# Turning C and x's last chunk with VectorE and DMAs instead of TensorE, in a gated mix of a state-space layer and an FFN

## The chip, the cores and the metric

The kernel runs on one core of one Trainium2 chip. The metric is the time of one execution on the device, in microseconds, the median of the runs shown. TensorE multiplies matrices into PSUM (eight banks), VectorE and ScalarE work on rows of 128 partitions, POOL (GpSimd) and SP (SyncE) mostly issue DMAs.

## The reference

For 2048 tokens x of width 448 (bf16):

```python
g = sigmoid((x * gate_w).sum(-1, keepdims=True))
Lam_bar = exp(dt * Lam);  B_bar = ((Lam_bar - 1) / Lam)[:, None] * Bmat        # complex
h = Lam_bar * h + B_bar @ x_t                                                  # for each token t
a = 2 * Re(h @ Cmat.T) + x * Dskip
b = silu(x @ w1) @ w2                                                          # 448 -> 1792 -> 448
out = g * a + (1 - g) * b
```

The recurrence over complex h is the only part that goes from token to token.

## The kernel before, in words

The tokens are worked in four chunks of 512 (`CH`), each of four blocks of 128. The 448 complex states lie in seven "slots" of 128 partitions: real parts of three blocks, a mixed slot 3 (64 real, 64 imaginary), imaginary parts of three blocks.

For a chunk tc, TensorE makes x turned by transposes (`x_transposes`, L498 to 518; the first chunk by `x0_transposes`), then two kinds of products with it (`x_products`, L647; all matmuls have line L663): F(tc), 14 tiles of x @ w1, and B(tc), 7 tiles of x with B. A product is cut into 64-row halves that run in pairs. `evict` (L623) takes them from PSUM: F by ScalarE with SiLU into aT, B into U (chunk 0 by VectorE, L640, the others by ScalarE, L642).

`lanes(tc)` (L706) is the recurrence, on VectorE: U is multiplied by COS and SIN (a rotation that turns the complex recurrence into a real one) into H; seven scans (L736) run along the tokens into Gf (float32); Gf is cast to bf16 back into U, by DMAs of POOL (L390) for chunks 0 to 2 and by ScalarE (L746) for chunk 3; then the rotation is undone into H (products with PO, COS; the final subtraction). The carry from chunk to chunk is `gin`.

`ffn2(tb)` (G, L765) multiplies aT by w2 for one block (L774), ScalarE scales it by 1 - g into fe (L780), and a POOL DMA adds it to Tb (L782), which is the x tile itself, holding g * x * Dskip by then. `readout(tb)` (C, L786) multiplies H by CP, seven matmuls (L795), and VectorE adds g times that to Tb (L798); SP stores the block (L801).

CP is C turned and scaled. `readout_weights(k)` turns it on TensorE (L814), ScalarE scales one copy into ct (L822, L825), and VectorE combines them from PSUM (L827, L830). `gates(tc)` (L834) makes g.

The order. `Plan` keeps all operations with what they read and write; `order` simulates them with a cost each and fixes each engine's queue beforehand. TensorE's queue is the order in which the program adds its operations. For the other engines the ready operation that can start first is taken, and of several the one with the lowest `prio`. SP also works in that planned order. Each engine runs its own queue in order, so a waiting instruction holds all behind it. TensorE's order is, with the readout weights as cp:

```python
F0 and B0, B1;  cp(0) G(0,1) cp(1,2) G(2,3) cp(3)
F1, one tile of F2, B2 (x chunk 2 turned in it);  G(4..7);  C(0..3)
rest of F2, B3, F3 (x chunk 3 turned in it);  C(4..7);  G(8..11);  C(8..11);  G(12..15);  C(12..15)
```

Buffers: there are four H (H2 first holds C as loaded, H3 first holds B), and two U, taken in turn by the chunks.

Of the kernel before, what the change touches and what calls it, by code (L numbers as in the profile page):

```python
# [24 lines left out]
NFILL = 2  # L25
XCOL = [0, 128, 256, 320]
# [22 lines left out]
class Op:  # L49
    __slots__ = ("i", "eng", "fn", "reads", "writes", "cost", "prio", "sem",  # L50
                 "deps", "succ", "ps_w", "ps_r", "start", "end", "bytes", "tag", "own")


class Plan:
# [5 lines left out]
    RATE = {"pool": 300e3, "hw": 300e3}  # L60
    LAP = {"dve": 0.08, "act": 0.09}
# [6 lines left out]
    def add(self, eng, fn, reads=(), writes=(), cost=0.2, prio=50, sem=None, nbytes=0, tag=""):  # L68
# [28 lines left out]
        o.own = False  # L97
        o.start = o.end = None
# [5 lines left out]
    def order(self):  # L104
# [14 lines left out]
        def earliest(o):  # L119
            t = 0.0  # L120
            for d in o.deps:
                p = ops[d]
                t = max(t, p.end + (self.HOP[p.eng] if p.eng != o.eng else 0.03))
            for x in o.ps_w:
                if x.bank is None:
                    b = place(x.n, t)
                    if b is None:
                        return None
                    t = max(t, max(banks[b:b + x.n]) + 0.1)
            return t  # L130
# [13 lines left out]
        while len(done) < len(ops):  # L144
# [5 lines left out]
            for eng, lst in cands.items():  # L150
# [9 lines left out]
                o = min((c for c in cand if c[0] <= t0 + 1e-9), key=lambda c: (c[1].prio, c[1].i))[1]  # L160
# [116 lines left out]
def bass_gated_mix__ssm_conv_s5__dense_activation_silu__prompt_kernel(nc, A_x, A_Lambda_re, A_Lambda_im, A_B_re, A_B_im, A_C_re, A_C_im,  # L277
               A_log_dt, A_Dskip, B_x, B_w1, B_w2, gate_w, out):
    with ExitStack() as ctx:
# [9 lines left out]
        xT = sb("xT", [128, 4, S_TOK], BF16)  # L289
# [3 lines left out]
        CP = sb("CP", [128, NSLOT, D_MOD], BF16)  # L293
        aT = [sb(f"aT{k}", [128, NFB, CH], BF16) for k in range(2)]
        UG = [sb(f"UG{k}", [128, 8, CH], BF16) for k in range(2)]
# [3 lines left out]
        H2C = sb("H2C", [128, 3840], BF16)  # L299
        H = [H2C[:, 0:3584].rearrange("p (s n) -> p s n", s=NSLOT) if k == 2 else sb(f"H{k}", [128, NSLOT, CH], BF16) for k in range(4)]  # L300
        Cnat = H2C[:, :].rearrange("p (b l) -> p b l", b=4)
        cnn = [f"H2_{s}" for s in range(7)] + ["H2_3i"]
# [91 lines left out]
        def load_w1(q, k, a, b):  # L394

            cols = slice(w1cuts[k], w1cuts[k + 1])
            src = B_w1[320:448, cols] if a == 3 else B_w1[128 * a:128 * b, cols].rearrange("(b p) f -> p b f", p=128)
            load(q, w1s[:, 3, cols] if a == 3 else w1s[:, a:b, cols], src, " ".join(f"w1_{k}_{i}" for i in range(a, b)),
                 256 * (b - a) * (cols.stop - cols.start))
# [11 lines left out]
        Bnat = H[3][:, :, 0:D_MOD]  # L411
        load("sp", Bnat[:, 0:3, :], A_B_re[0:384, :].rearrange("(b p) d -> p b d", p=128), "H3_0 H3_1 H3_2", 384 * 896)
        load("sp", Bnat[0:64, 3, :], A_B_re[384:448, :], "H3_3", 64 * 896)
        load("sp", Bnat[64:128, 3, :], A_B_im[384:448, :], "H3_3i", 64 * 896)
        load("sp", Bnat[:, 4:7, :], A_B_im[0:384, :].rearrange("(b p) d -> p b d", p=128), "H3_4 H3_5 H3_6", 384 * 896)
        btn = {s: [f"BT{s}_{h}" for h in range(2)] for s in range(7)}
        load_w1("sp", len(w1cuts) - 2, 0, 3)
        load_w1("sp", len(w1cuts) - 2, 3, 4)
# [8 lines left out]
        def load_C():  # L427

            for h in range(2):
                rows = lambda a: a[224 * h:224 * h + 224, :].rearrange("(b p) l -> p b l", p=56)  # L430
                to = Cnat[64 * h:64 * h + 56]
                load("sp", to[:, :, 0:448], rows(A_C_re), f"Cn0{h} " + (" ".join(cnn) if h == 0 else ""), 224 * 896)
                load("sp", to[:, :, 576:960], rows(A_C_im[:, 0:384]), f"Cn1{h}", 224 * 768)
                load("sp", to[:, :, 448:512], rows(A_C_im[:, 384:448]), f"Cn2{h}", 224 * 300)
                load("sp", to[:, :, 512:576], rows(A_C_re[:, 384:448]), f"Cn3{h}", 224 * 300)

        load_xn(1)
        load("sp", w2s[:, :, :], B_w2.rearrange("(fb p) d -> p fb d", p=128), "w2", F_FF * 896)
        load_C()
# [28 lines left out]
        def x0_transposes(q0, part, who):  # L468
# [12 lines left out]
            for h in range(2):  # L481
                src = lambda h=h: bk(tk, h).bitcast(BF16)[:, 0:256].rearrange("p (q b n) -> p q b n", q=2, n=64)
                dst = xT[:, q0:q0 + 2, 256 * part:256 * part + 256].rearrange("p q (b h n) -> p q b h n", h=2, n=64)[:, :, :, h, :]
# [11 lines left out]
        xn_of = {tc: {q: [f"xT{tc}_{h}" for h in range(2)] for q in range(4)} for tc in range(1, NCH)}  # L495
        xn_of[0] = {q: [f"xT0_{q}{part}{h}" for part in range(2) for h in range(2)] for q in range(4)}

        def x_transposes(tc, who):  # L498
# [13 lines left out]
            for h in range(2):  # L512
                src = lambda h=h: bk(tk, h).bitcast(BF16).rearrange("p (q b n) -> p q b n", q=4, b=4)
                dst = xT[:, :, tc * CH:(tc + 1) * CH].rearrange("p q (b h n) -> p q b h n", h=2, n=64)[:, :, :, h, :]
                if who[h] == "d":
                    DVE(lambda e, src=src, dst=dst: e.tensor_copy(dst, src()), [tk], [f"xT{tc}_{h}"], 0.69, 2.2, "xTe")
                else:
                    ACT(lambda e, src=src, dst=dst: e.activation(dst, src(), AF.Copy), [tk], [f"xT{tc}_{h}"], act_cost(1024), 2.2, "xTe")

# [73 lines left out]
        def b_transposes(s0, s1, who):  # L593
# [12 lines left out]
            PE(mm, [f"H3_{s}" for s in range(s0, s1)] + ["H3_3i"] * (s0 <= 3 < s1) + ["ident"], [tk], n * 4 * 0.0285, "BT")  # L606
# [16 lines left out]
        def evict(pair, tk):  # L623

            kinds = [t[0] for t in pair]
            for k, n in ((0, 2),) if pair[0][:2] == pair[-1][:2] and len(pair) == 2 else ((0, 1), (1, 1))[:len(pair)]:
# [10 lines left out]
                U, un = UG[tc % 2], f"U{tc % 2}_"  # L637
                dst = U[:, sl, :]
                if tc == 0:
                    DVE(lambda e, src=src, dst=dst: e.tensor_copy(dst, src()), [tk], [f"{un}{m}" for m in names], 0.15 + 0.53 * n, 2.6, "U")  # L640
                else:
                    ACT(lambda e, src=src, dst=dst: e.activation(dst, src(), AF.Copy), [tk], [f"{un}{m}" for m in names], act_cost(512 * n), 5, "U")  # L642
# [4 lines left out]
        def x_products(tiles, fill={}, wait=()):  # L647
# [10 lines left out]
            def steps(k, h, a, z):  # L658
                def body(pe):
                    for n, cut in list(enumerate(part[h]))[a:z]:  # L660
                        for b, ((i, p0), tile) in enumerate(zip(cut, pairs[k])):
                            tc = tile[1]
                            r = pe.matmul(bk(toks[k], b), weights(tile, p0, p0 + 64, i), xT[p0:p0 + 64, i, tc * CH:(tc + 1) * CH],  # L663
# [42 lines left out]
        def lanes(tc):  # L706
            pr = 20 + tc
            A, an = H[tc], f"H{tc}"
            U, u = UG[tc % 2], f"U{tc % 2}_"
            Gb = U  # L710
            t = f"L{tc}"
            if tc == 0:
# [20 lines left out]
            for s in (3, 0, 4, 1, 5, 2, 6) if tc else (0, 4, 1, 5, 2, 6, 3):  # L733
# [34 lines left out]
        def ffn2(tb):  # L768
# [13 lines left out]
            P.add("pool", lambda e: e.dma_start(Tb[:, tb, :], f[:, :], accum_op=ALU.add), [fn, f"Tb{tb}"], [f"Tb{tb}"], 0.94, 2, sem(), 115000, tag="Tb+")  # L782

        outs = [sem() for _ in range(NOT)]

        def readout(tb):  # L786
# [3 lines left out]
            for n, (a, b) in enumerate(cuts):  # L790
                tk = Ps()

                def mm(pe, tk=tk, a=a, b=b):
                    for s in range(NSLOT):
                        r = pe.matmul(bk(tk)[:, 0:b - a], H[tc][:, s, o:o + 128], CP[:, s, a:b], start=(s == 0), stop=(s == NSLOT - 1))  # L795
                    return r
                PE(mm, [f"H{tc}_{s}" for s in range(7)] + [f"CP{s}" for s in range(NSLOT)], [tk], NSLOT * (0.0025 + (b - a) / 2400), f"C{tc}")
# [5 lines left out]

        def readout_weights(k):

            tk = Ps(2)

            def mm(pe):
                for j, c0 in ((0, 128 * k), (1, 448 if k == 3 else 576 + 128 * k)):
                    for b in range(4):  # L810
                        o = j * 224 + 56 * b
                        for h in range(2):
                            p = slice(64 * h, 64 * h + 56)
                            r = pe.transpose(bk(tk, h).bitcast(BF16)[:, o:o + 56], Cnat[p, b, c0:c0 + 128], ident[p, p])  # L814
                return r
            PE(mm, [f"Cn{n}{h}" for n in range(4) for h in range(2)] + cnn + ["ident"], [tk], 8 * 0.0285, "CT")
            both_banks = lambda j: bk2(tk).rearrange("p h n -> p (h n)").bitcast(BF16).rearrange("p (h n) -> p h n", h=2)[:, :, 224 * j:224 * j + 224]
            re = lambda: both_banks(0)
            im = lambda: both_banks(1)
            in_two = lambda a: a.rearrange("p (h n) -> p h n", h=2)  # L820
            c, cn = ct[k % 2], f"ct{k % 2}"
            ACT(lambda e: e.activation(in_two(c[:, 0, :]), im(), AF.Copy, scale=sc2[:, k:k + 1]), [tk, "sc2"], [cn + "a"], act_cost(448, 1), 3, "ct")  # L822
            both = [cn + "a"]
            if k < 3:
                ACT(lambda e: e.activation(in_two(c[:, 1, :]), re(), AF.Copy, scale=sc2[:, k:k + 1]), [tk, "sc2"], [cn + "b"], act_cost(448, 1), 3, "ct")  # L825
                both.append(cn + "b")
            DVE(lambda e: e.scalar_tensor_tensor(in_two(CP[:, k, :]), re(), sc1[:, k:k + 1], in_two(c[:, 0, :]), ALU.mult, ALU.add),  # L827
                [tk, "sc1"] + both, [f"CP{k}"], 0.68, 1, "CP")
            if k < 3:
                DVE(lambda e: e.scalar_tensor_tensor(in_two(CP[:, 4 + k, :]), im(), nsc1[:, k:k + 1], in_two(c[:, 1, :]), ALU.mult, ALU.add),  # L830
                    [tk, "sc1"] + both, [f"CP{4 + k}"], 0.68, 1, "CP")

        def gates(tc):
# [3 lines left out]
               xnn + ["gwb"] + (["Gf0"] if tc else []), ["xg"], 1792, 19, "xg")  # L837
            tt(xnat[:, b4, :], xnat[:, b4, :], dkb[:, None, :].to_broadcast([128, 4, D_MOD]), ALU.mult,
               xnn + ["dkb"] + (["Gf0"] if tc else []), [f"xd{tc}"] + xnn, 1792, 19, "xd")
# [21 lines left out]
        def C(*tbs):  # L861
# [6 lines left out]
                   {(1, 0): [parameters], (K - 2, 0): turn_b[:1], K - 2: turn_b[1:2], K - 1: turn_b[2:], 7: xt(1, "da") + [lambda: lanes(0)]}, [K - 2])  # L868
# [3 lines left out]
        for f in cp(0) + G(0, 1) + cp(1, 2) + G(2, 3) + cp(3):  # L872
            f()
        x_products(F(1) + F(2, 0, 1) + B(2), {2: xt(2, "aa")})
# [44 lines left out]
```

## Time and profile before

| | |
|---|---|
| median of 3 runs | 141.26 us (141.24 to 141.38) |
| the profiled execution: its own time, its span | 141.25 us, 139.5 us |
| granted TensorE clock | 0.998 |
| TensorE, matmuls busy | 135.9 us |
| VectorE, ScalarE, POOL busy | 122.0, 90.3, 39.2 us |
| the chain that ended last: TensorE's share | 97% |
| DMA traffic | 14.71 MB, mean 105 GB/s |

The page gives busy time of each engine, the span in 40 slices with the busy tenths of each, and the chain of work that ended last, followed back from the last instruction. The trace behind it gives each engine's instructions in order of time, with the idle time ahead of an instruction and what ended it. "x16" counts instructions of a group; L814 is a line of the kernel.

### The profile page before, as it was taken

The numbers are of one execution on the slowest core, as the hardware profiler recorded it, in microseconds if no ns is written. First come the engines' busy times: TensorE is split into PE (matmuls) and PEld (weight loads), VectorE is DVE, ScalarE is ACT, GpSimd is POOL, SyncE is SP. The second block draws the span as 40 slices with busy tenths as digits, with TensorE's granted clock in tenths as the row PEclk, the third lists the DMA queues.
The fourth block names the chain that finished last, engine by engine and source line by source line (L and its number), as shares of the span: only waits on it lengthen the run. The fifth ranks groups of instructions, "written<-read, shape, count | busy, mean of one in ns | idle before, by whom it ended". The sixth has DMA issues, their size and how long they took to land.

```text
span 139.5 us, 3000 instructions
## 1 busy us (share of the span) xinstructions
PE 135.9 (97%) x1201; PEld 67.0 (48%) x1201; DVE 122.0 (87%) x179; ACT 90.3 (65%) x157; POOL 39.2 (28%) x72
## 2 busy tenths in 40 slices
PE   7999999999999999999999999999999999999992
PEld 2445454455544544455544544444455555555561
DVE  0319999999999999999999999999999999997053
ACT  3349768999989999823694887799931268312300
POOL 7134040100248440227733001824000314022220
PEclk9999999999999999999999999999999999999999
DMA  4998999510156770104976200674202322323242
GB/s 136 337 294 243 363 320 238 177 42 0 31 79 94 129 110 1 38 15 73 157 131 155 38 5 0 95 133 79 38 4 97 66 33 36 83 83 61 40 94 71
DMA packets 17956, 14.71 MB, mean 105 GB/s; under 512 B 2835, under 2 KB 17814, under 8 KB 17942
## 3 DMA queue, kind: packets, MB, share of 16 engines
q0 software_dynamic: 6064, 5.51, 24.8%
q1 hardware_dynamic: 11318, 8.65, 20.7%
q10 hardware_dynamic: 560, 0.36, 0.8%
q8 instruction: 9, 0.15, 0.4%
q14 instruction: 5, 0.04, 0.1%
HBM read 7.17 MB, written 1.84 MB: 65 GB/s over the span
## 4 chain that ended last, share of the span: by engine, by line
PE 97%; DVE 0%; issue 0%
PE ps L663 46%; PE ps L774 31%; PE ps L795 15%; PE ps L463 2%; PE ps L508 1%; PE ps L478 1%; PE ps L814 1%; PE ps L604 1%; DVE ot L798 0%; PE ps L675 0%; PE ps L464 0%; PE ps L536 0%
## 5 line engine op out<-in xcount | busy, mean ns | idle before, releaser
L663 PE MATMUL ps<-xT,w1s 64*128 64x512 bf16 x392 | 48.5, 378 | 0.0
L774 PE MATMUL ps<-w2s,aT 128*128 128x448 bf16 x224 | 43.2, 353 | 0.0
L634 ACT ACTIVATE aT<-ps 128x1024 bf16<-128x1024 f32 (+1 forms) x30 | 28.7, 969 | 8.5 <-PE ps L663 8.4
L774 PEld LDWEIGHTS ps<-w2s,aT 128*128 128x128 bf16 x224 | 21.7, 98 | 20.4 <-ACT xnat L849 0.4
L663 PEld LDWEIGHTS ps<-xT,w1s 64*128 64x128 bf16 x392 | 19.7, 94 | 22.3 <-DVE xT L486 0.7
L663 PE MATMUL ps<-xT,BT 64*128 64x512 bf16 x196 | 25.8, 376 | 0.0
L782 POOL DMA_DIRECT2D xnat<-fe x16 | 14.1, 900 | 37.9 <-ACT fe L780 37.2
L780 ACT ACTIVATE fe<-ps,g 128x448 bf16<-128x448 f32 x16 | 10.1, 632 | 21.1 <-PE ps L774 21.0
L390 POOL DMA_DIRECT2D UG<-Gf x27 | 14.7, 549 | 20.9 <-DVE Gf L736 20.4
L736 DVE TENSOR_TENSOR_SCAN Gf<-rc,gin,H 128x512 f32<-128x512 f32 x14 | 17.2, 1268 | 0.0
L795 PE MATMUL ps<-CP,H 128*128 128x448 bf16 (+2 forms) x98 | 16.4, 326 | 0.0
L663 PEld LDWEIGHTS ps<-xT,BT 64*128 64x128 bf16 x196 | 10.8, 94 | 11.1 <-DVE Gf L562 0.2
L798 DVE SCALAR_TENSOR_TENSOR ot<-ps,g,xnat 128x448 bf16<-128x448 f32 (+2 forms) x18 | 10.8, 622 | 6.0 <-issue 4.6
L390 POOL DMA_DIRECT2D UG<-UG x8 | 4.8, 597 | 29.2 <-ACT UG L642 17.4
L704 DVE TENSOR_TENSOR H<-UG,COS 128x3584 bf16<-128x3584 bf16 (+4 forms) x10 | 12.6, 1266 | 0.0
L795 PEld LDWEIGHTS ps<-CP,H 128*128 128x128 bf16 x98 | 8.9, 98 | 7.5 <-DVE k L752 0.4
L642 ACT ACTIVATE UG<-ps 128x1024 bf16<-128x1024 f32 (+1 forms) x12 | 10.7, 923 | 1.4 <-PE ps L663 1.4
L842 ACT ACTIVATE junk<-xg 128x448 bf16<-128x448 bf16 x16 | 9.2, 574 | 2.1 <-DVE xg L704 2.0
L849 ACT ACTIVATE xnat<-xnat,g 128x448 bf16<-128x448 bf16 x16 | 9.8, 671 | 0.2
L704 DVE TENSOR_TENSOR PI<-UG,SIN 128x512 bf16<-128x512 bf16 (+2 forms) x13 | 9.1, 722 | 0.0
L704 DVE TENSOR_TENSOR PO<-UG,SIN 128x1536 bf16<-128x1536 bf16 (+1 forms) x8 | 8.7, 1087 | 0.1
L736 DVE TENSOR_TENSOR_SCAN Gf<-rc,gin,H2C 128x512 f32<-128x512 f32 x7 | 8.5, 1265 | 0.0
(102 smaller groups left out, 126.5 us busy)
## 6 DMA issues: line engine op xcount, KB each, us to landing
UG<-Gf POOLq DMA_DIRECT2D x21, 128.0 KB, 2.5
xnat<-fe POOLq DMA_DIRECT2D x16, 112.0 KB, 2.6
out_dram<-ot SPq DMA_DIRECT2D x15, 112.0 KB, 1.7
w2s<-in_B_w_dram SPq DMA_DIRECT2D x1, 1568.0 KB, 11.8
xnat<-in_A_x_dram SPq DMA_DIRECT2D x3, 448.0 KB, 6.1
w1s<-in_B_w_dram SPq DMA_DIRECT2D x1, 576.0 KB, 6.2
UG<-UG POOLq DMA_DIRECT2D x8, 64.0 KB, 2.2
H2C<-in_A_C_re_dram SPq DMA_DIRECT2D x2, 196.0 KB
```

The lines of the kernel that those rows point to most:

```text
L390: P.add(q, lambda e: e.dma_start(dst, src), list(after), name.split(), 0.6 if q == "pool" else 0.5, prio, sem(), nbytes, tag="ld " + name)
L634: ACT(lambda e, src=src, dst=dst: e.activation(dst, src(), AF.Silu), [tk, "tbl"], [f"aT{tc % 2}_{m}" for m in names], act_cost(512 * n), 2 ...
L642: ACT(lambda e, src=src, dst=dst: e.activation(dst, src(), AF.Copy), [tk], [f"{un}{m}" for m in names], act_cost(512 * n), 5, "U")
L663: r = pe.matmul(bk(toks[k], b), weights(tile, p0, p0 + 64, i), xT[p0:p0 + 64, i, tc * CH:(tc + 1) * CH], start=(h == 0 and n == 0), stop=( ...
L704: DVE(lambda e: e.tensor_tensor(o, a, b, op), r, w, dve_cost(n, 2), prio, tag)
L736: DVE(lambda e, s=s, b=b, init=init: e.tensor_tensor_scan(Gf[:, s, :], rc[:, b:b + 1].to_broadcast([128, CH]), A[:, s, :], init, ALU.mult, ...
L774: r = pe.matmul(bk(tk)[:, 0:D_MOD], aT[tc % 2][:, fb, o:o + 128], w2s[:, fb, :], start=(fb == 0), stop=(fb == NFB - 1))
L780: ACT(lambda e: e.activation(f[:, :], bk(tk)[:, 0:D_MOD], AF.Copy, scale=g1[:, tb:tb + 1]), [tk, f"g1_{tc}"], [fn], act_cost(448, 1), 7, "fe")
L782: P.add("pool", lambda e: e.dma_start(Tb[:, tb, :], f[:, :], accum_op=ALU.add), [fn, f"Tb{tb}"], [f"Tb{tb}"], 0.94, 2, sem(), 115000, tag= ...
L795: r = pe.matmul(bk(tk)[:, 0:b - a], H[tc][:, s, o:o + 128], CP[:, s, a:b], start=(s == 0), stop=(s == NSLOT - 1))
L798: DVE(lambda e, tk=tk, a=a, b=b: e.scalar_tensor_tensor(ot[tb % NOT][:, a:b], bk(tk)[:, 0:b - a], g[:, tb:tb + 1], Tb[:, tb, a:b], ALU.mul ...
L849: ACT(lambda e, tb=tb: e.activation(Tb[:, tb, :], xnat[:, tb, :], AF.Copy, scale=g[:, tb:tb + 1]), [f"xd{tc}", f"g_{tc}"], [f"Tb{tb}"], ac ...
```

## The change

- C is loaded as it lies (128 rows a block, the last block of 64 padded by a memset of POOL, six loads, ahead of w2 instead of behind it). VectorE turns its 32x32 blocks, four instructions, into the third U buffer, and 16 DMAs of SP put the blocks in place in CP. `readout_columns` does this. TensorE's transposes of C (L814) are gone.
- `x_blocks(3)` does the same for x's last chunk: four VectorE instructions into H2, 16 DMAs. Chunks 0 to 2 are turned by TensorE as before, chunk 1 one pair of products earlier.
- `readout_weights` scales CP in place, from SBUF. ScalarE's part of it may be planned from 59 us on (`CTAT`), with a priority below that of the second FFN outputs.
- C(0..3) move behind F3. After it: C(4..7), G(8..13), C(8..11), G(14,15), C(12..15).
- Blocks 4 to 11: ScalarE scales the readout by g into ct, a POOL DMA adds it to Tb, SP stores Tb, in place of VectorE's L798.
- Three U buffers and three H, taken in turn; B is loaded into U2. Chunk 3 thus uses U0 and H0.
- Chunk 0's lanes use the four large products of the other chunks. Gates get priorities of their own. The last part of w1 is loaded as two halves of two blocks each, and xT is laid out by chunks.

The core of the diff:

```diff
-        H = [H2C[:, 0:3584].rearrange("p (s n) -> p s n", s=NSLOT) if k == 2 else sb(f"H{k}", [128, NSLOT, CH], BF16) for k in range(4)]
+        H = [sb(f"H{k}", [128, NSLOT, CH], BF16) for k in range(3)]
-        UG = [sb(f"UG{k}", [128, 8, CH], BF16) for k in range(2)]
+        UG = [sb(f"UG{k}", [128, 8, CH], BF16) for k in range(3)]
-        load_w1("sp", len(w1cuts) - 2, 0, 3)
-        load_w1("sp", len(w1cuts) - 2, 3, 4)
+        load_w1("sp", len(w1cuts) - 2, 0, 2)
+        load_w1("sp", len(w1cuts) - 2, 2, 4)
+        POOL(lambda e: e.memset(Cnat[:, 3, :], 0.0), [], ["Cnz"], 0.9, 5)
         load_xn(1)
+        load_C()
         load("sp", w2s[:, :, :], B_w2.rearrange("(fb p) d -> p fb d", p=128), "w2", F_FF * 896)
-        load_C()
...
+        def x_blocks(tc):
+            X32 = (xT[:, 3, :, :] if tc == 2 else H[2][:, 0:4, :]).rearrange("p m (q b i) -> p m q b i", q=4, i=32)
...
+            for k, (q0, q1, c, b0, b1) in enumerate(((0, 3, 0, 0, 2), (0, 3, 0, 2, 4), (3, 4, XCOL[3], 0, 2), (3, 4, XCOL[3], 2, 4))):
...
+                DVE(lambda e, dst=dst, src=src: e.transpose(dst, src), [f"xn{tc}"] + names[0:k][0:1], [names[k]] + cnn * (tc == 3 and k == 0), 0.15 + 256 * n / 960, XPRIO[tc], "xTd")
+            for g in range(4):
+                for m in range(4):
+                    to = xT[32 * m:32 * m + 32, tc, :, :].rearrange("p q (b g i) -> p (q b) g i", b=4, i=32)[:, :, g, :]
+                    P.add("sp", lambda e, to=to, g=g, m=m: e.dma_start(to, X32[32 * g:32 * g + 32, m, :, :, :].rearrange("p q b i -> p (q b) i")),
+                          names + held, [f"xT{tc}_{g}{m}"], 0.68, 400, k, 150000, tag="xTm")
...
+                if tb in OUTA:
+                    ACT(lambda e, tk=tk, f=f: e.activation(f, bk(tk)[:, 0:D_MOD], AF.Copy, scale=g[:, tb:tb + 1]),
+                        [tk, f"g_{tc}"], [fn], act_cost(448, 1), 3, "out")
+                    P.add("pool", lambda e, f=f: e.dma_start(Tb[:, tb, :], f, accum_op=ALU.add), [fn, f"Tb{tb}"], [f"Tb{tb}"], 0.94, 2, sem(), 300000, tag="Tb+")
+                    P.add("sp", lambda e: e.dma_start(out2[t0:t0 + 128, :], Tb[:, tb, :]), [f"Tb{tb}"], [], 0.3, 1, outs[NOT], 128 * 896, tag="st")
+                    continue
...
+        def readout_columns():
+            C32 = UG[2][:, 0:NSLOT, :].rearrange("p s n -> p (s n)").rearrange("p (m t b i) -> p m t b i", m=4, b=4, i=32)
...
+            for b in range(4):
...
+                DVE(lambda e, dst=dst, src=src: e.transpose(dst, src), [f"Cn{n}" for n in range(6)] + ["Cnz"] + [CBEH] * (CBEH != "") + cnn + turned, [names[b]],
+                    0.15 + 896 / 960, CPRIO, "CTd")
+            for g in range(4):
+                for m in range(4):
+                    to = CP[32 * m:32 * m + 32, :, :].rearrange("p t (b g i) -> p (t b) g i", b=4, i=32)[:, :, g, :]
+                    P.add("sp", lambda e, to=to, g=g, m=m: e.dma_start(to, C32[32 * g:32 * g + 32, m, :, :, :].rearrange("p t b i -> p (t b) i")),
+                          names + held, [f"CT{g}{m}"], 0.75, 400, k, 300000, tag="CTm")
...
-        for f in cp(0) + G(0, 1) + cp(1, 2) + G(2, 3) + cp(3):
+        for f in G(0, 1, 2, 3):
             f()
+        for f in cp(0, 1, 2, 3):
+            f()
...
-        for f in G(4, 5, 6, 7) + C(0, 1, 2, 3):
+        for f in G(4, 5, 6, 7):
             f()
-        x_products(F(2, 1) + B(3) + F(3), {1: xt(3, "aa"), 9: [lambda: gates(3), lambda: lanes(3)]})
-        for f in C(4, 5, 6, 7) + G(8, 9, 10, 11):
+        x_products(F(2, 1) + B(3) + F(3), {1: xt(3, "aa") if 3 not in XBLK else [], 9: [lambda: gates(3)]})
+        for f in C(0, 1, 2, 3):
             f()
-        for f in C(8, 9, 10, 11) + G(12, 13, 14, 15) + C(12, 13, 14, 15):
+        lanes(3)
+        for f in C(4, 5, 6, 7) + G(8, 9, 10, 11, 12, 13) + C(8, 9, 10, 11) + G(14, 15) + C(12, 13, 14, 15):
             f()
```

The constants that the change sets: `XBLK = (3,)`, `OUTA` blocks 4 to 11, `L0M = True`, `CPRIO = 15`, `CPP = 20.5`, `CTAT = 59.0`, `GPR = (14, 20.3, 21.5, 19)`, `XPRIO[3] = 20.2`.

## The prediction

> **What bounds the kernel now.** I read the busy times first, then the slices of the span, then the chain of work that ended last. All three name TensorE.
>
> ```profile
> span 139.5 us, 3000 instructions
> ...
> PE 135.9 (97%) x1201; PEld 67.0 (48%) x1201; DVE 122.0 (87%) x179; ACT 90.3 (65%) x157; POOL 39.2 (28%) x72
> ...
> PE   7999999999999999999999999999999999999992
> ...
> DVE  0319999999999999999999999999999999997053
> ```
>
> The reader is to see two full rows. TensorE has no slice below 9 between the first and the last. VectorE has none between about 10 and 127 us, and falls to 0 just before the end: an engine with little room left. The chain, in order of time (start, length, what), shows what TensorE does:
>
> ```profile
> 28.31 0.21 PE ps L814 x16
> 28.51 5.40 PE ps L774 x28
> 33.92 0.52 PE ps L814 x32
> 34.44 5.40 PE ps L774 x28
> 39.84 0.31 PE ps L814 x16
> ...
> 57.24 10.70 PE ps L774 x56
> ...
> 73.24 3.99 PE ps L663 x36
> 77.23 0.47 PE ps L508 x32
> 77.70 21.80 PE ps L663 x202
> 99.50 5.40 PE ps L795 x28
> ```
>
> L814 are C's transposes and the L508 at 77.23 those of x's last 512 tokens: both lie on the chain, with no wait around them. Last, VectorE's timeline near the end, where the last H is made (subtraction of PO) for the readouts that start at 131.38:
>
> ```profile
> 124.07 2.09 DVE L704 TENSOR_TENSOR H<-UG,COS 128x2048 bf16<-128x2048 bf16 x2
> 126.07 2.09 DVE L704 TENSOR_TENSOR H<-H,PO 128x2048 bf16<-128x2048 bf16 x2
> 132.80 0.69 DVE L798 SCALAR_TENSOR_TENSOR ot<-ps,g,xnat 128x448 bf16<-128x448 f32 x1 [4.64 <-issue]
> ```
>
> H is complete at 126.07 + 2.09 = 128.16. From 10.89 to there that timeline shows no idle time, so VectorE's chain is 3.2 us shorter than TensorE's, and no more.
>
> **TensorE's sum.** Removed: L814, 0.21 + 0.52 + 0.31 = 1.04 us, and L508 once, 0.47: 1.51. Two joints go too: the FFN outputs cut by L814 take 5.40 + 5.40 = 10.80, uncut 10.70 (at 57.24): 0.10; the L663 stretch cut at 77.23 takes 25.79 for 238 matmuls, where 56 uncut ones took 6.04, so 25.67: 0.12. Between 0 and 0.22 for the joints I take 0.14. Nothing is added to TensorE; the first readouts (5.30 us, 28 matmuls) only move. The profiled execution took 141.25 us (span 139.5 and 1.75 around it; the median of the runs shown is 141.26, the same). Sum: 141.25 - 1.51 - 0.14 = 139.60, if nothing else is late.
>
> **TensorE's new dates.** C4 to C7 began at 99.50. With 1.65 removed and C0 to C3 moved behind F3, F3 ends at 99.50 - 5.30 - 1.65 = 92.55, C3 at 97.85, C7 at 103.15, G13 (six at 2.65) at 119.05, C11 at 124.35, G15 at 129.65; C12 starts at about 129.7. Chunk 3's first B product, at 82.07 before, comes at 82.07 - 5.30 - 1.65 = 75.1.
>
> **VectorE's sum.** Added: four transposes 128x896 for C, two 128x768 and two 128x256 for x, 5632 elements a partition. No such instruction is in the trace. Rows at one element a step: the CAST from PSUM takes 1216 ns for 1024 and 682 for 512, so 1.04 ns an element and 148 ns, and a next instruction starts about 80 ns before a record ends. That gives 1.00 us for 896, 0.87 for 768, 0.34 for 256: 4.0 + 1.7 + 0.7 = 6.4 us. From below: the bf16 products, 2006 ns for 3584 (0.52 ns an element), 3.5 us. From above: the scan, 1265 ns for 512 (2.3 ns an element), 13 us. I take 6.4: a transpose has one input and no chain from element to element, as the CAST, and 32 lanes must be collected, so I don't grant it the packed rate.
>
> Removed: eight output instructions L798 (token blocks 4 to 11) at 0.59 from start to start: 4.7. Chunk 0's 18 small products and sums (3 x 0.60 + 15 x 0.335 = 6.8) become chunk 1's four (1.93 + 0.87 + 1.14 + 1.95 = 5.9): 0.9. The seven CP instructions stay and move later; they read SBUF instead of PSUM, where I find no row and grant between 0 and 0.06 each, so I take 0. Net: 6.4 - 4.7 - 0.9 = +0.8, so H would be complete at 129.0, against 129.7. **Slack 0.7 us**, where it was 3.2: this is the price of the edit that costs nothing while covered. A waiting VectorE delays its whole queue, the final H last, and TensorE's C12 behind it, one for one.
>
> Does VectorE stay without gaps? The new wait is chunk 3's first product: H has three buffers, so it writes H0, which C3 releases at 97.85 (before, it ran at 96.35). Queued behind it is all of chunk 3, some 18 us; in front lie chunk 2's tail and four outputs, about 9 us, and by the sum above VectorE reaches it only about 101 to 105. It costs nothing there. The tails that wait for the float-to-bf16 casts by DMA (2.5 us to landing) are filled by the next chunk's first products (5.9 us), as now.
>
> **Queues and transfers.** C is turned after chunk 0's gate products (they ended at 26.4 before), so about 27 to 31.5. Its 16 DMAs are issued by SP, which sat idle from 23 to 70. Issues of C's loads took 0.54 to 0.88 us, so 16 take 9 to 14: until 41 to 46, and some 2 us to land. Each carries 896 pieces of 64 bytes; 16 of them give 896 pieces to each DMA engine. The trace's packet records have 13 ns for 128 bytes and 9 ns for 4 (hardware queue), so 64 bytes take about 11: 10 us, hidden under the issues. Upper end: the page's queue 1, 11318 packets in 20.7% of 16 engines' 139.5 us, is 41 ns a packet of 764 bytes: 37 us, landed at 69. C's pieces are in U2, which B2's evictions need at about 53 (54.3 before), and the scaling waits on ScalarE from about 59. x's 16 follow (turned about 45 to 48 in chunk 0's cast gap): landed at about 62, needed at 75.1, and H2, their source, is wanted by chunk 2's first product, which is later than its 60.96 of before. All covered, with 6 us or more.
>
> w2 now goes behind C's loads. It landed at 10.07 + 11.8 = 21.9; C's 0.8 MB at the 350 to 380 GB/s seen between 14 and 20 us puts it 2.3 later, 24.2, needed at 28.3. x1 is turned one pair (1.5 us) earlier, about 18, and landed by 9.59 + 7.1 = 16.7. w1's last loads, split evenly, end by about 13.7, needed at 16.45. The memset of C's padding falls into POOL's 4.95 us of idle time before 9.30. All cost 0.
>
> ScalarE loses two x evictions (1.9) and gains eight scalings (0.63 each) at 99 to 104 and 120 to 125, where its timeline has idle pieces of 5.13 and 2.02. Moving the ct work (seven, 0.64 each) from 28 to 41 to 59 and later takes it from a full stretch to one with 1.3 to 2.1 us holes. POOL gains eight issues (0.86); SP stores wait for them: C11's end 124.35 + 0.63 + 0.86 + 2.6 + 1.7 = 130.1, ahead of the end at about 138. Three U buffers take away waits that nothing on the chain had: 0.
>
> **A rule against this change.** The packet row above (13 ns for 128 bytes) stands first. The Trainium skill, VectorE: DVE Perf Modes, "The three transpose paths", says that a plain DMA copy that does a transpose by strides is 19 times slower than the crossbar's when the innermost destination stride is large. By that, an estimate for C would be 0.92 MB at 350 GB/s (2.6 us) times 19, 50 us; no run here shows it, and here the inner run is 64 bytes dense. The rival that it gives is worked out from rows below.
>
> **The rivals.** (1) *VectorE is late at the last H* (slower). Place: the wait of C12. Price: what VectorE takes above +0.8, less 0.7 of slack, added to the time. It stalls TensorE from 0.7 us on and makes the kernel slower than before from 0.7 + 1.65 = 2.35 us on, that is from transposes at 8.8 us or as much in gaps. At the scan's rate: 13 - 6.4 - 0.7 = 5.9, so 145.5. For it: slack 0.7 of 118 us, and an instruction with no row. Against: nothing in the rows with one input is as slow as the scan.
>
> (2) *The 64-byte pieces are slow.* At 41 ns the scaling could start at 69, just after TensorE enters F2 at 67.94 - 1.14 = 66.8, whose evictions queue on ScalarE behind the waiting scaling; eight banks hold about 6 us of products. So TensorE stalls from 66.8 + 6 - 31.5 = 41.3 us for 896 pieces on, 46 ns each, and every further ns costs 0.9 us: 60 ns would give 152. For: no SBUF-to-SBUF row at this size. Against: 9 and 13 ns.
>
> (3) *The gain is hidden anyway:* a late w2 (from 28.3 on) or x3 holds TensorE by as much as it saved: 141.2. Against: slacks of 4 and 13 us.
>
> **How the numbers follow.** The forecast, 139.60 with its own range 139.35 to 139.85: 0.62. Rival 1 in part (stall 0.25 to 1.4, 139.85 to 140.97): 0.10. Rivals 1 and 3 within 0.2% of before (140.97 to 141.53; 0.2% is about what a measurement of this kernel can tell from no change): 0.08. Rival 1 above that, 141.5 to 145.5: 0.14. Rival 2, 142 to 152: 0.06. So faster 0.72, same 0.08, slower 0.20. The range reaches from 139.3 to 142.0, which leaves out the upper part of rivals 1 and 2, about 0.17.
>
> **What would show it.** TensorE's chain without L814 and with two L508 pieces, F3's end near 92.5, C12 near 129.7 with no idle time before it, G0 near 28.1. VectorE: transposes near 1.08, 0.95 and 0.42 us; last H near 129.0; no gaps from 11 on. C's DMAs landed before 48, x3's before 65. Wrong would be idle time of TensorE before C12 (rival 1), before F2's evictions (rival 2), before G0 or B3 (rival 3).

## The result, and the profile after

The changed kernel takes 143.17 us (142.62 to 143.78), the one before 141.49 us beside it: a ratio of 1.0121 [1.01, 1.0143]. It is slower, by 1.7 us, where 1.65 us less was forecast, and the time lies above the range. Medians here and below leave out the few slow executions, those over 1.5% above the fastest of the same kernel. The profiled execution took 143.31 us. Its page begins with the same rows as the one of before:

```profile
span 141.5 us, 2839 instructions
...
PE 135.1 (95%) x1105; PEld 65.6 (46%) x1105; DVE 122.7 (87%) x165; ACT 93.6 (66%) x164; POOL 46.5 (33%) x81
...
PE   7999999999999996999999999999999999999691
...
DVE  0318999999999639999999999999999999999562
```

TensorE has less to do and VectorE 0.7 us more, as forecast. But VectorE's row now has a hole (6, 3) in its 14th and 15th slices, some 46 to 53 us, TensorE's has a 6 behind it, and both have a low digit near the end. The chain that ended last no longer runs back to the start through TensorE; it is followed only as far as C12, which waits:

```profile
132.88 4.16 PE ps L839 x21
```

VectorE's timeline shows the hole (start, length, line, what, and in brackets the idle time ahead and what ended it):

```profile
47.29 0.42 DVE L555 STREAM_TRANSPOSE H<-xnat 128x256 bf16<-128x256 bf16 x1
...
47.68 0.59 DVE L796 TENSOR_TENSOR k<-Gf,SS 128x3 f32<-128x3 f32 x4
51.78 0.96 DVE L748 TENSOR_TENSOR PO<-UG,SIN 128x1536 bf16<-128x1536 bf16 x1 [3.51 <-DMA UG<-Gf]
...
53.09 1.05 DVE L748 TENSOR_TENSOR xg<-xnat,gwb 128x1792 bf16<-128x1792 bf16 x1
```

PO is the first product that undoes chunk 0's rotation. It reads U after the casts that POOL's DMAs make (UG<-Gf), and waits 3.51 us for the last one that it needs, the fifth of nine. Before, the same place of VectorE's timeline had a large product in front, and no wait:

```profile
48.32 2.00 DVE L704 TENSOR_TENSOR H<-UG,COS 128x3584 bf16<-128x3584 bf16 x1
...
50.94 0.96 DVE L704 TENSOR_TENSOR PO<-UG,SIN 128x1536 bf16<-128x1536 bf16 x1
```

The casts are also slower. The DMA issues between 26 and 52 us (count, KB each, median us from issue to landing), first before, then after:

```profile
UG<-Gf POOLq DMA_DIRECT2D x7, 128.0 KB, 2.3
```

```profile
CP<-UG SPq DMA_DIRECT2D x16, 56.0 KB, 3.6
UG<-Gf POOLq DMA_DIRECT2D x7, 128.0 KB, 5.2
```

C's 16 DMAs are issued from 31.07 to 47.01 and land 2.3 to 7.8 us later, the casts are issued from 41.57 on. POOL's issue of a cast takes 0.53 us at the median before and after; it is the transfer that takes longer. The cast that PO needs was issued 4.48 us ahead of PO before (46.46 and 50.94) and landed after 2.20. Now it is issued at 45.43, VectorE is free for PO at 48.27, 2.84 us later, and it lands after 6.22. In two-microsecond stretches (busy time of PE, PEld, DVE, ACT, POOL; clock; DMA share; GB/s) before had this for 48 to 50:

```profile
48.00:50.00 2.00, 2.00 (x22) 0.92 (x20) 2.00 (x2) 2.00 (x3) 1.41 (x4) 1.00 0.66 107
```

and after, the DMA share stays above 1 from 42 to 52 while VectorE and ScalarE run dry:

```profile
46.00:48.00 2.00, 2.00 (x22) 0.88 (x18) 1.97 (x7) 2.00 (x3) 0.86 (x2) 1.00 1.16 158
48.00:50.00 2.00, 2.00 (x22) 0.93 (x20) 0.24 (x2) 1.69 (x3) 1.23 (x3) 1.00 1.16 158
50.00:52.00 2.00, 2.00 (x22) 0.92 (x20) 0.22 (x1) 0.96 (x1) 0.00 (x0) 1.00 1.12 141
```

How the hole reaches TensorE: chunk 1's gate product xg stands behind PO on VectorE; ScalarE waits for it, with evictions behind it; TensorE waits for the eviction. One line of ScalarE's timeline, then two of TensorE's:

```profile
54.17 0.58 ACT L902 ACTIVATE junk<-xg 128x448 bf16<-128x448 bf16 x1 [3.21 <-DVE xg L748]
```

```profile
55.81 2.33 PE L707 MATMUL ps<-xT,BT 64*128 64x512 bf16 x20 [1.38 <-ACT aT L677]
...
132.88 5.50 PE L839 MATMUL ps<-CP,H 128*128 128x448 bf16 x42 [1.07 <-DVE H L748]
```

The second wait is the same hole at the other end of VectorE's queue: the last H is complete at 132.83. **The sum.** In the chain of before C12 begins at 131.38. Removed from TensorE 1.50 (below); a start that came 0.38 later (the last matmul of B1 ends at 28.69 instead of 28.31); lost at B2 1.56 (that stretch ends at 58.14, and without a wait its pieces would end at 56.58) and at C12 1.06: 131.38 - 1.50 + 0.38 + 1.56 + 1.06 = 132.88. From there to the end of the span it takes 8.62 instead of 8.12, and 1.81 instead of 1.75 lies around the span: +1.50 + 0.50 + 0.06 = 2.06 = 143.31 - 141.25.

### The profile page after: what moved, and what is told of

It is laid out like the page before. It is cut to its first block, busy times and chain, and to the rows that moved or that the text cites. A ratio compares the mean times of both kernels' runs of the same rounds, so it can differ in the third digit from the quotient of the medians.

```text
span 141.5 us, 2839 instructions
## 1 busy us (share of the span) xinstructions
PE 135.1 (95%) x1105; PEld 65.6 (46%) x1105; DVE 122.7 (87%) x165; ACT 93.6 (66%) x164; POOL 46.5 (33%) x81
## 2 busy tenths in 40 slices
DMA packets 41684, 17.00 MB, mean 120 GB/s; under 512 B 25539, under 2 KB 41542, under 8 KB 41670
## 5 line engine op out<-in xcount | busy, mean ns | idle before, releaser
L780 DVE TENSOR_TENSOR_SCAN Gf<-rc,gin,H 128x512 f32<-128x512 f32 x21 | 25.5, 1264 | 0.1
L826 POOL DMA_DIRECT2D xnat<-fe x16 | 15.4, 961 | 29.3 <-ACT fe L824 23.1
L406 POOL DMA_DIRECT2D UG<-Gf x27 | 15.4, 586 | 23.1 <-DVE Gf L780 22.7
L839 PE MATMUL ps<-CP,H 128*128 128x448 bf16 (+2 forms) x126 | 21.7, 332 | 1.1 <-DVE H L748 1.1
L839 PEld LDWEIGHTS ps<-CP,H 128*128 128x128 bf16 x126 | 11.6, 98 | 11.3 <-DVE H L748 1.5
L748 DVE TENSOR_TENSOR H<-UG,COS 128x3584 bf16<-128x3584 bf16 (+2 forms) x9 | 16.1, 1807 | 0.0
L748 DVE TENSOR_TENSOR PI<-UG,SIN 128x1536 bf16<-128x1536 bf16 (+1 forms) x8 | 8.4, 1083 | 0.0
L849 DVE SCALAR_TENSOR_TENSOR ot<-ps,g,xnat 128x448 bf16<-128x448 f32 (+2 forms) x10 | 5.6, 582 | 3.0 <-issue 1.6
L748 DVE TENSOR_TENSOR H<-H,PO 128x3584 bf16<-128x3584 bf16 (+2 forms) x5 | 8.1, 1644 | 0.0
```

What stands on the lines that cost most here:

```text
L406: P.add(q, lambda e: e.dma_start(dst, src), list(after), name.split(), 0.6 if q == "pool" else 0.5, prio, sem(), nbytes, tag="ld " + name)
L748: DVE(lambda e: e.tensor_tensor(o, a, b, op), r, w, dve_cost(n, 2), prio, tag)
L780: DVE(lambda e, s=s, b=b, init=init: e.tensor_tensor_scan(Gf[:, s, :], rc[:, b:b + 1].to_broadcast([128, CH]), A[:, s, :], init, ALU.mult, ...
L839: r = pe.matmul(bk(tk)[:, 0:b - a], H[tc % 3][:, s, o:o + 128], CP[:, s, a:b], start=(s == 0), stop=(s == NSLOT - 1))
```

## The experiments

**The theories.** Theory 1: C's transfers and chunk 0's casts use the same DMA engines at the same time, and the casts land late. Theory 2: it is VectorE's order alone, PO stands directly behind the casts. Theory 3: VectorE has too much work anyway, and the hole only shows where. Ratios are to the kernel before on the same chip.

**e1_few: C's DMAs with a seventh of the pieces.** The rest of CP is zero (POOL clears it early), so six sevenths of C are left out.

```diff
-                    to = CP[32 * m:32 * m + 32, :, :].rearrange(...)
+                    to = CP[32 * m:32 * m + 32, 0:1, :].rearrange(...)
```

> C's 16 DMAs stay in their places but carry one slot of seven (128 pieces of 64 bytes instead of 896 each); the other six slots of CP are zero, so most of C is left out. VectorE's, ScalarE's and TensorE's queues are those of the changed kernel. Theory 1 (C's transfers share the DMA engines with chunk 0's casts, which land after 4.7 to 6.2 us instead of 2.2 to 2.7, and VectorE waits 3.5 us for them): casts land after 2.2 to 2.8, VectorE's gap before the first PO at 48 to 52 is below 0.3 us, TensorE's stalls before B2's last products (1.4) and before C12 (1.1) are gone, time 140.3 to 140.8. Theory 2 (the gap comes from VectorE's order alone, PO being placed right behind the last casts): gap 3 to 3.5 us and 143.2 as before. Theory 3 (VectorE has too much work anyway, the gap is not what makes the last H late): gap gone, but C12 still waits 1 us or more, 141.8 to 142.5.

Measured: 140.66 us, 0.991 [0.9882, 0.9938]. Six of the nine casts land after 2.4 to 2.8 us, three in a row after 4.4, 3.6 and 3.1. The stall at B2 is gone. The hole is 0.87 and C12 waits 0.36, where below 0.3 and no wait were expected:

```profile
49.10 0.96 DVE L749 TENSOR_TENSOR PO<-UG,SIN 128x1536 bf16<-128x1536 bf16 x1 [0.87 <-DMA UG<-Gf]
```

VectorE has the same order, and C's DMAs carry fewer bytes: 2.64 of the 3.51 us are C's transfers. The 0.87 that stay need two things. PO stands 2.83 us behind the issue of the cast that it needs (45.40, and VectorE is free at 48.23), and that cast took 3.58 us, though all of C's pieces had landed by 43.16. With the 2.20 of before PO would not have waited even in this order. What held the cast is not shown. The trace's DMA records have a load of instructions, 16 KB, from 45.76 to 47.41, while it was under way; in e2 and e6 such a load (from 46.70 and 47.40) also falls within the cast that PO needs (3.84 and 3.33 us), in the changed kernel too (49.45), and before in none that PO needed.

**e2_early: C turned and sent 6 us earlier.** `CPRIO` goes from 15 to 2.9; VectorE turns C from 20 us on.

> One constant: C's four transposes on VectorE go ahead of the last phase work (planned at 20 to 25 us instead of 26 to 30); chunk 0's lanes start at the same planned time as before. All of C is moved. Theory 1: the 16 DMAs are issued from about 25 to 37, before most of the casts (41.5 to 48.7); the casts land after 2.3 to 3.5 us, gap below 1 us, time 140.4 to 141.2. Theory 2: gap 3 to 3.5, 143.2. Theory 3: gap gone, C12 still late by 1 us or more, 141.8 to 142.5.

Measured: 141.49 us, 0.9981 [0.9953, 1.0008], above the 140.4 to 141.2 that were expected. C's DMAs are issued from 25.3 to 37.9, most in 0.66 us, and land after 2.3 at the median, the last at 40.36. The casts are issued from 41.48 on and still take 3.4 at the median; the hole is 1.13, C12 waits 0.53, and nothing at B2. The bytes are the same as in the changed kernel, only at another time. Beside the changed kernel's in e5, the median span is 2.3 us shorter (139.35 and 141.65), the time 2.0; up to 2.9 us lay outside the span here, which stays unexplained.

**e3_late: chunk 0's products behind chunk 1's.** An earliest planned date for three operations; only VectorE's order changes.

```diff
+            if tc == 0:
+                pq.at, pa.at, po.at = 51.3, 52.8, 53.5
```

> The transfers stay as in the changed kernel; only VectorE's order differs: chunk 0's products with PO and COS after the casts may be planned from 51.3, 52.8 and 53.5 us on, so that chunk 1's gate products and its first product run in the gap. Theory 1: casts still land after 4.7 to 6.2 us, but VectorE has other work; gap below 0.7 us, ScalarE no longer waits 3.2 us for the gate product, no stall at B2, C12 waits below 0.4: 140.3 to 141.0. Theory 2 gives the same here. Theory 3: gap gone, C12 still waits 1 us or more, 141.8 to 142.5.

Measured: 140.58 us, 0.9903 [0.9877, 0.9929]. The casts are as slow as in the changed kernel, and nobody waits for them. VectorE's timeline:

```profile
49.20 1.08 DVE L748 TENSOR_TENSOR xg<-xnat,gwb 128x1792 bf16<-128x1792 bf16 x1
50.20 2.02 DVE L748 TENSOR_TENSOR H<-UG,COS 128x3584 bf16<-128x3584 bf16 x1
52.13 1.08 DVE L748 TENSOR_TENSOR xnat<-xnat,dkb 128x1792 bf16<-128x1792 bf16 x1
53.13 0.95 DVE L748 TENSOR_TENSOR PO<-UG,SIN 128x1536 bf16<-128x1536 bf16 x1
```

and its DMA issues between 26 and 52:

```profile
UG<-Gf POOLq DMA_DIRECT2D x7, 128.0 KB, 5.1
```

So theories 1 and 2 are not rivals: late casts cost nothing with other work in front of PO, and PO so near behind the casts costs only what a cast takes above some 2.8 us: 0.87 without C's backlog.

**e4_x_on_tensore: x's last chunk turned by TensorE again.** `XBLK = ()`; VectorE has 2.8 us of transposes less, and SP no DMAs for x.

> x's last chunk is turned by TensorE as before (0.5 us more on TensorE, 2.3 us less on VectorE, 16 DMAs fewer); C as in the changed kernel. Theory 1: x's transfers came after the casts, so the casts are late as in the changed kernel and the gap is 2.5 to 4 us; the stall at B2 stays (1 to 2 us), the one before C12 goes, time 142.0 to 143.0. Theory 2 the same gap. Theory 3: with 2.3 us less of work the last H is in time, 141.0 to 141.8.

Measured: 141.41 us, 0.9969 [0.9943, 0.9995]; 142.0 to 143.0 were expected. The profiled execution took 142.40, a long one among these runs.

```profile
52.63 0.96 DVE L748 TENSOR_TENSOR PO<-UG,SIN 128x1536 bf16<-128x1536 bf16 x1 [3.26 <-DMA UG<-Gf]
```

Less work doesn't close the hole: theory 3 falls as a cause of it. It moves the loss. Chunk 1's gate product now stands ahead of PO (47.72), and TensorE loses nothing at B2, against the expectation. The last H comes at 130.42 and C12 doesn't wait. But TensorE stalls 0.76 us at B3: ScalarE had waited 3.27 us for VectorE's scaling of CP and 2.33 for chunk 2's gate product, with evictions behind both.

**e5_changed_again: the changed kernel once more**, on the chip of the next three.

> The changed kernel itself once more, beside the others of this call: ratio to the kernel before 1.010 to 1.014, VectorE's gap at 48 to 52 between 3 and 4 us, C12 waiting about 1 us. If the gap were chance (a transfer that happened to be late), it would be below 2 us here and the ratio near 1.00.

Measured: 143.52 us, 1.0136 [1.0112, 1.016], with a hole of 3.09, a stall of 0.96 at B2 and 1.33 at C12. The picture repeats.

**e6_four: C's DMAs with four sevenths of the pieces.** The edit of e1 with `0:4`; three sevenths of C are zero.

> As e1, with four slots of seven instead of one (512 pieces a DMA); three slots of CP are zero, so part of C is left out. Theory 1 (the bytes that C's DMAs put between the casts): casts land after 3 to 5 us, gap between those of e1 (0.9) and the changed kernel (3.5), about 1.5 to 2.5; ratio 0.998 to 1.006. Were it the 16 issues or the mere presence of a second queue, the gap would be as in e1; were it a threshold, as in the changed kernel.

Measured: 141.29 us, 0.9973 [0.9951, 0.9995]; a hole of 0.61, less than with one seventh. The expected 1.5 to 2.5 was wrong: the delay is not proportional to the bytes. With four sevenths most issues take 0.63 us, the last goes out at 42.2 and lands by 45.4, and the casts take 2.8 at the median. With all seven, issues grow from 0.66 to 2.2 us and the last goes out at 44.8, with a backlog that lands up to 7.8 us later. The backlog begins before the casts: issues slow from 36.05 on, when the first two FFN outputs' adds to Tb (issued at 34.70 and 35.77) are under way. C's pieces alone keep the DMA share at 0.68 to 0.69 (e2, 32 to 36 us), and the changed kernel's share is 1.26 at 38 to 40. So the reading that fits is that a backlog forms when the adds, and then the casts, ask for more than what C's pieces leave. The share alone doesn't tell a late cast: it reaches 1.20 in e6, too.

**e7_shared_pipe: one DMA pipe in the planner.** The planner simulated SP's and POOL's DMAs in separate pipes, and had put PO at 47.62 and the cast that it needs at 47.10.

```diff
-                q = "pool" if o.eng == "pool" else "hw"
+                q = "hw"
```

> One word in the planner: the transfers of POOL and of SP fill one pipe in its simulation instead of one each. Nothing else is changed; VectorE's planned order then has chunk 1's gate products and its four first products ahead of chunk 0's PO. Theory 1: casts land as late as in the changed kernel (4 to 7 us), gap below 0.5 us, no stall at B2 and C12, ratio 0.988 to 0.994. If the planner's wrong forecast of the landing isn't the cause of the order that waits, the gap stays and the ratio is above 1.005.

Measured: 140.54 us, 0.9944 [0.9909, 0.9979], at the edge of the expected 0.988 to 0.994. With one line the planner by itself finds an order with chunk 1's products ahead of PO, as in e3, and more of them. There is no hole at 48 to 52, and no stall:

```profile
49.68 2.02 DVE L748 TENSOR_TENSOR H<-UG,COS 128x3584 bf16<-128x3584 bf16 x1
51.62 1.08 DVE L748 TENSOR_TENSOR xnat<-xnat,dkb 128x1792 bf16<-128x1792 bf16 x1
52.62 2.09 DVE L748 TENSOR_TENSOR PI<-UG,SIN 128x1536 bf16<-128x1536 bf16 x2
```

**e8_early_and_late: e2 and e3 together.**

> Both edits of e2 and e3: C's DMAs 6 us earlier, and chunk 0's products planned later. Casts land after 2.6 to 4.5 us, no gap, TensorE without stalls: in the span as e3, 138.5 to 139.0; ratio 0.988 to 0.993. If the extra time that e2 shows beyond its span comes with the early transfers, the ratio is 0.993 to 0.998 and the part outside the span above 2 us.

Measured: 140.58 us, 0.9935 [0.9914, 0.9957], between the two expected ranges. No hole at the casts; the last H comes at 129.06, and C12 doesn't wait for it. The chain runs through TensorE again:

```profile
28.41 10.70 PE ps L820 x56
39.11 5.50 PE ps L707 x50
...
67.00 25.79 PE ps L707 x238
...
129.98 3.99 PE ps L841 x21
```

No faster than e3 or e7: once the hole is gone, TensorE sets the time. And of e2's extra time outside the span little is here: 1.8 us lie outside at the median, and 2.5 at most.

**e9_before_again: the kernel before, with a profile of its own.**

> The kernel before, unchanged, with a profile of its own, for its start stretch. The runs of changed kernels so far have shown TensorE's first second-FFN group at 28.35 to 29.44 us, with a wait of 0.7 to 1.9 us for weights in F0, where the first profile of before had 0.70 us. Theory: the start varies by chance from execution to execution, whatever the kernel. Then this run may show another wait than 0.70 us there too, and what follows the start stretch has the same lengths as before within 0.1 us. Rival: the changed order of loads makes it late. Then this run shows 0.70 us again.

Measured: 141.57 us, span 139.8. The wait in F0 is 0.99 us (0.70 in the first profile), and the last matmul of B1 ends at 28.63 (28.31). From there C12 begins 103.08 us later (103.07). So a start 0.32 later, nearly the changed kernel's +0.38, comes by chance in the unchanged kernel too. Whether the new order of loads has a part in it is not shown; in the runs with the change B1 ends at 28.41 to 29.51.

**e10_slack: e8 and 1.93 us of useless work for VectorE.**

```diff
+                if tc == 3:
+                    tt(PI[:, :, :], COS[:, :, :], SIN[:, :, :], ALU.mult, cosn + sinn, pin, 3584, pr, t)
```

> e8_early_and_late with one useless product more on VectorE: 128x3584, COS times SIN into PI, queued in chunk 3's part ahead of its own first product, 1.93 us. It tests the price that the prediction gave: VectorE's work above its slack comes back one for one. e8 had the last H complete at 129.06 and C12 at 129.81, so 0.7 us of slack. By that price the last H comes at about 131.0, TensorE waits 1.2 us at C12, and the time is e8's 140.60 + 1.2 = 141.8. Rival: VectorE has holes somewhere behind the added product that swallow it; then the last H stays below 129.8, C12 doesn't wait, and the time stays at 140.6.

Measured: 142.58 us, 1.0068 [1.0036, 1.0099], where 141.8 was expected. The line of the wait in TensorE's timeline, and VectorE's last H:

```profile
131.53 5.50 PE L843 MATMUL ps<-CP,H 128*128 128x448 bf16 x42 [1.52 <-DVE H L748]
```

```profile
129.39 2.08 DVE L748 TENSOR_TENSOR H<-H,PO 128x2048 bf16<-128x2048 bf16 x2
```

The last H is complete at 131.47, 2.41 us later than in e8 (1.94 the product, 0.45 chunk 1's PO, whose last cast landed late, at 78.65, and the start 0.03). TensorE was ready at 130.01 and waits 1.52 us. In e8's chain C12 began at 129.98 (its record starts at 129.81, while the matmul ahead still runs), 0.92 behind the last H; 2.41 - 0.92 = 1.49. So the price holds, one for one above the slack. The profiled time went up by 142.25 - 140.55 = 1.70: 0.18 more than the wait goes to the restart, since VectorE's last piece ends 5.90 us behind C12's begin after a wait, in the changed kernel too, and 5.72 without one. By the ratios the medians of e8 and e10 lie 1.9 us apart, 0.2 more than the two profiles.

## Why the prediction was wrong, point by point

- **TensorE's sum was right but for the joints.** In e3, e7 and e8, which have no stall, the chain takes 101.56 to 101.57 us from G0 to C12 (28.41 to 129.98 in e8), where 131.38 - 28.31 = 103.07 lay between them before: 1.50 removed, 1.65 forecast. The transposes' 1.51 went as forecast; the joints' 0.14 did not come. Behind the uncut G0 to G3 the F1 stretch takes 5.50 instead of 5.40, and the uncut L663 stretch 25.79, just what its two pieces took (3.99 + 21.80).
- **VectorE's sum was right.** Its transposes take 1.07 to 1.10, 0.97 and 0.42 to 0.44 us (1.08, 0.95, 0.42 forecast). The last H, less the late start (0.10 to 0.86), came at 128.96 to 129.34 in those three, against 129.0.
- **The step that failed:** "The tails that wait for the float-to-bf16 casts by DMA (2.5 us to landing) are filled by the next chunk's first products (5.9 us), as now." Both halves were wrong. The landing time was taken from rows in which C's transfers did not run, though the same prediction has SP issuing them "until 41 to 46, and some 2 us to land", over the first dates of the casts; measured, 5.2 us. And the fill was taken for a property of the code, though VectorE's queue is fixed by a planner that the change gives new dates. Before, only one of the next chunk's four first products (2.0 us) stood ahead of PO; after, none did, and VectorE was free for PO 2.84 us behind the issue of the cast that it needs. The prediction itself spoke of "chunk 0's cast gap" and put x's transposes there, but three of the four came ahead of it (35.81, 38.61 and 47.29) and the fourth behind PO (52.73). 129.0 + 0.38 + 3.51 = 132.89; the last H came at 132.83.
- **"All covered" asked the wrong question.** It asked whether C's pieces come in time for those who need them, and they did. It did not ask whom they hold up. A row of before could have warned: "Issues of C's loads took 0.54 to 0.88 us" leaves out the first and the last of the eight, which took 5.37 and 1.20, at a DMA share of 1.00 (10 to 20 us). The Trainium skill, DMA: Bandwidth & Descriptors, "Queues, rings and completion order", says that each DMA engine goes round the queues that have work for it, a packet at a time. By that, casts and C's pieces take turns on the same engines; casts at 5.2 instead of 2.3 us agree, and so does e1, though no record names the packet that a cast waited behind.
- **Rival 1 came, by its second door.** It had the place (C12) and the price (above 0.7 of slack, one for one; slower than before from 2.35 us on, "or as much in gaps"), and e10 bears the price out. It was held unlikely because only the transposes' duration was weighed. It left out that a hole near 50 us stops TensorE twice: at once through ScalarE (1.56), then through the last H (1.06). The first doesn't add to the second: C12 begins 0.05 behind the last H, whatever TensorE lost before.
- **Rival 2 is out.** C's and x's 22,528 pieces of 64 bytes (the page's packets under 512 bytes went from 2,835 to 25,539) took 8 ns each at the median, against 11 forecast. The 19 times of the Trainium skill (VectorE: DVE Perf Modes, "The three transpose paths") don't arise at this size: where 50 us was the estimate, C's 16 DMAs took 15.1 us in e2 from the first issue to the last landing. Rival 3 is out too: w2 landed at 24.4 and G0 began at 28.69, and TensorE did not wait at B3.
- **The tail was left out.** From VectorE's last piece to the end of the span it takes 2.72 us (138.78 to 141.5; 2.75 to 2.85 in e3, e7, e8), and 2.40 before (137.10 to 139.5). The second-last store goes out 0.71 us after its piece is written (139.12 against 138.41), before it was 0.29. With the joints this is why the best variants' median span is 1.1 to 1.2 us below that of before (138.7 to 138.8, and 139.9) and not 1.65. Its cause wasn't followed and stays open.

## What to carry to other kernels

A transfer that is hidden from its own reader can still delay another transfer's reader: lay the dates of all DMAs over each other, whatever engine issues them, and don't take a landing time from a stretch that was quiet. Where a queue is fixed by a planner, "filled as now" has to be read from the new order, and a planner that gives each issuer a pipe of its own can put an instruction right behind a transfer that shares its engines. One line of the model (e7) was worth as much here as moving the work by hand.

## What the runs showed of the hardware

- A cast from float to bf16 by DMA of 128 KB took 2.3 us to land in the kernel before and 5.2 us beside C's backlog. SP's own issues of 56 KB slowed as well, from 0.66 to 2.2 us.
- The slowing is not proportional to the bytes: 8 and 32 KB in each of C's 16 DMAs left the casts at 2.8 us at the median, 56 KB made it 5.2. No size between 32 and 56 was run.
- The wait for weights at the start of F0 was 0.70 and 0.99 us in two profiles of one kernel, and moved all that follows by 0.32.
